# One due time and nineteen of twenty-eight lines of TensorE's written order in a window attention kernel

## The chip, the core and the metric

The kernel runs on one core of a Trainium2 chip. A core has a matrix engine (TensorE, PE in the profile, with its weight loads as PEld), a vector engine (VectorE, DVE), an engine for activation functions (ScalarE, ACT), a general engine (GpSimd, POOL) and a sequencer that here only issues transfers (SyncE, SP). They run side by side and wait for one another with semaphores. TensorE writes to PSUM, eight banks of 128 partitions by 512 words of 32 bits. The metric is the time of one execution on the device, in microseconds (us); lower is better.

## The reference

The input is an image of 224 x 224 points with 96 channels. The first 48 channels attend within horizontal strips of 8 rows, the last 48 within vertical strips of 8 columns. There are 28 strips each way, each of 1792 points.

```python
qkv = einsum('bhwc,cd->bhwd', x, wqkv)          # q, k, v of 96 channels
# first 48 channels: windows of 8 rows
ah = softmax(einsum('bqc,bkc->bqk', qh, kh) * 48 ** -0.5)
oh = einsum('bqk,bkc->bqc', ah, vh)
# last 48 channels: windows of 8 columns
av = softmax(einsum('bqc,bkc->bqk', qv, kv) * 48 ** -0.5)
ov = einsum('bqk,bkc->bqc', av, vv)
o = einsum('bhwc,cd->bhwd', concat(oh, ov), wo)
```

## The kernel before, in words

**Tiles.** The kernel takes two strips at a time: a pair `P`, 0 to 13 for rows and 14 to 27 for columns (`NPH` is 14, so pair 14 is the first column pair). In a pair the queries are cut into chunks `c` of 512, 512, 512 and 256, the keys into 14 groups of 128. A tile is 128 keys by 512 queries of both strips, 1024 columns; a pair has 14 + 14 + 14 + 7 = 49 tiles. Keys stand on the partitions, so the exponentials of a tile go into the next product as they are, and a column of ones beside the values gives the sum that softmax divides by.

**Two ways to an exponential.** 40 or 41 tiles of a pair have it taken by ScalarE (line 876, one instruction for a tile, 1126 in all). Their scores go by turns into banks 0, 1 and banks 2, 3, so TensorE can write the scores of a tile only after ScalarE has read the tile two before it. The other 8 or 9 tiles of a pair (246 in all) go through a polynomial: VectorE reads the scores (line 1003, for some tiles also 1005), GpSimd squares (lines 1016, 1019, 1020), TensorE computes the same scores a second time, and VectorE puts the result together (line 1008). These scores lie in the ring, banks 4 to 7, which also holds the sum over the values that is being added up, the projections and the output products.

**The written order.** TensorE runs its steps in the order of 28 strings, `ORDER`, one for each pair; the string of pair P is line 46 + P. A letter is a step:

- `q`: the scores of the next tile for ScalarE (line 700, 4 matmuls);
- `1`, `3`: the first scores of a polynomial tile, `2`, `4` the second (line 713). `3` and `4` take two neighbouring banks of the ring and VectorE reads both in one instruction of 1024 columns; `1` and `2` take any two banks and VectorE reads them with two instructions of 512;
- `v`: one tile of exponentials times the values (line 726), summed in one ring bank over a chunk; VectorE then copies the sum out (line 893);
- `k`: a step that prepares a pair ahead: its keys (lines 530 and 535), a small product for a bias of the queries (557 and 561), its queries (530 and 544) and its values (575 and 582); `K` is two such steps with one copy;
- `g`: an output product of the column half (lines 644 and 650); `f`: one of the last pair (611, 618 and 623).

Steps `q`, `1` to `4` and `f` are said to be of one kind here, `v`, `k` and `g` of the other, because TensorE takes longer from a step of one kind to one of the other.

**Who orders the rest.** A planner in the kernel's own program goes through the letters, keeps a time for each engine, and so decides the order of VectorE's, GpSimd's and SyncE's instructions (`dve_step`, `pool_step`, `do_s`, `do_fill`). It only sets the order. On the chip each engine runs its list in that order and each instruction waits by semaphore for what it reads and overwrites.

**The sums turned over.** Of a column pair the sums lie with channels on the partitions. After the copies of chunks 1 and 3 of a column pair, `turn_ot` (line 424) puts a transposing transfer on SyncE's queue: the first turned part has 8 groups of 128 points, the second 6. When the planner thinks that a part has landed, it gives VectorE the reciprocals of the sums of that part (`emit_rn`, line 965; 16 columns for the first part, 12 for the second), and after that GpSimd the multiplication (line 980). The second part's `turn_ot` stands in SyncE's queue behind the transfers that are queued at the start of the next pair: `rows_in` (line 444) and `plan_x` (line 465, the points of the pair after the next). The due time is this line:

```python
dq.append(dict(what="rn", ready=tm["sp"] + TURN, dur=0.16 if c == 1 else 0.135, P=P, z=c // 2))
```

`TURN` is 4.5 us; `c == 1` is the first part, `c == 3` the second.

Of the kernel before, what the change touches and what calls it, by code (L numbers as in the profile page):

```python
# [44 lines left out]
ORDER = [
    "qqkkkqkq3q1qkq1qkqkqvv3qvvq1qvqkqvvq2vq2vq3qkvqvqvvkq2qkkqvvvv1qkvqv1qkvqvkq4vqvvq4vqvkq4vqkq1vvqkqkvkqv1qvq2vqvkkv",
    "qq2vvq1qvvqvvq1vqvvvq1qvvqvvvqvq2vqkvvqkq2vq4qvvkq1vqvqvkvvq1qkvqvv2qvvq4vqvkq4qvvkq3qkvvq1qvkvqvqv2qvvqvkvq3qvkvvq1qkvvv",
    "q2vq2qvq1vqvvqvvvq1vq1qvvqvvvq4qvkqv4qvkqv4qvkqv3qkvqvvvqkvq1q4vqkvvq3qkvq2qkvq2qvkqv1qvvqvvqv4qvvkq1qvvvqkvq4vqvkvq1v",
    "q2qvvq1vqvvqvvvvq1vqv1qvqvqkq4vqkvq1vqvkvqvvq4qvvvkq2qvv1qvvq2qvvq1vkq4qvvkq3qvqkvqvvq1vvq4qvkqv3qvvvq2qkvqkkvqv2qkvqv2",
    "qvvq1vqvvqvvq2vvqv2qvvq1vqvq4vkqvq1vqkvqvvqkq1vkqvvqvvq2vqkvvqkq3vvqkq2vqkq2vq3qkvq1qvvqvvq1qvv3qkqvv2qvvqkvqvkvq2vq",  # L50
    "v1qvqvvvq2vqq1vvqvv1qvvqvqv2qq4vqvkq1vqvvvqvq1vqkvkqkvvq2kqv3qkvqv4qvvqkq1vqvvvqkqvv4qvqkv2qvvq2vqv1qvq4vqvvqkvkvq1qkvvq2v",
    "vq1qvvqvvq1vvqvq1vqvvqvv3qvvqvvqvkq2qv1qvqkv2qkvqvq2vvq1qkvvvq2kqq4vqvkq1vvqkqvvq4qkvqv1qvq4vkqvq3vkqvvq3qkvqvvqvvkvq",
    "2qvv1qvvq2vq3qvvqvvqvvq1vqvvvqkqvkvq1qvvkqv2qkvqv2qkvvq1vqv4qvkqvvq2vq4qvvkq1qvkvqvvqv2qvvq2qvv3qvkqv1qvvqkvq4vqvkvq4qvvvkq1",
    "qvvqvvq2vvqvvq1vq2qvvvq1qvvqvq1vkqvvqvkqvkqv2qkvqv2qkq1vqvvq2vqv2qvkvqkq1vqv1qvqvvvqv1qkqvvvq1qkvq2qvkqv2qvvvq1kqvvqk",
    "vqvvq2vvq4qvvvvq1vqvq4vqvkq1qvvqvvvq2vqv1qvvqvkqvkqvvvq2q1qvvq1vvqkvq2vkqv3qkvqvvqvqkq4vqkq3vqvvq4vqkvqk2qvvq1vqvvkq2qkv",
    "vq1vqvvvqq2vqvvq1vvqvvqkkq4qvkqv3qvkvqvqvvkq4vqkq1vqvkqvvq3qkvqv1qvqkvkq2qvvq2vvq2qvvq1vqvvvqv1qvvq2qvvq4vqkvq4vqvkvq1v",
    "vq1qvvvqvvqv1qvq2vvq3qvvqvvqkq1vqvvvqv2qkqvv2qkqkvvq2vkqv3qvvqv3qvkqvq2vvq2qvkqkvq1qvkqvvvqvvq3vqkvq4vqkvq2qvv2qvvq3vqvkv",
    "q1vqvqvvqvkvq2vqv1qvvq1qvkqvvvq2qvvq1vqkqvvvq2qvq3kqvq1vkqvkq2qvkqvkq2vqv4qvkqv1qvvqvvvq4qvvvqk3qkqvv4qkvqv2qvq1vkqv1",
    "qvvqvvq1qvv1qvqvvvq4qvvvqv4qvqkv2qvq1vqvvqvkqkvq3vqkvq1kvq2qvvvq4qkvvqv1qkvqvqvvq2vvq1qvkqv2qkvqvvvq3vqvkqkq2vvq1qkvvqvv",
    "qv2qvvq1vvq3qvvvqv2qvq2qvvkq2vqvv1qkvqvqv3qvvvvq4qkvvvqkvq2kqvv3qvkqvqvkqv3qvvkq4qvvvkq2qvvvq1vqvkqv1qkvvqvvq1qvvvq2qkvvvq4qvvvvq",  # L60
    "1qvvvvggqqkvvkq4vqkvq1vkqvkq4qvvvq4qvgqv3qvkqvvq2kqvgvqv1qvq2vqv3qkvqvvvqvgq1qv1qvvgqgq2qkvvq2qvgvqvkq1vqvgqvvqv2qvkqvvvq2vqk",
    "vvq1vqgvq1qvv2q2qvqvv1qvvqvgqkqvkvq4qkvqvvgq1vkqvvqk3qvgq3qvvvqvkqvq2vvq2qvvvq2qvv3qvqk4qvvqkqkvq2qvkgqvkq3qvgvqv1qkvqv",
    "vq2qvvqggqvvvq1gqvvvq3qvvkq2q4qvvvkvq1qvvvvqvq1vvq1qvkgqvkqv2qkvqggqvkq2vvq1qvvvqvkvq4qvkqv4qvvvq3qkvvvq4qkvvvqkq1vvq4qvvkvq3q",
    "vvvqvvgqvq1vvq1qvv2qvqgvgqkq2vvqkkqv2qvkqvgq1vvqvvqv3qvvqk4qvvqkvq4vqvgvq4qvvkq1qvvqvvq1vqvvvq1vvq2qvgvqkq2vqkkqkvvqkvgq1qvvvqvvqv",
    "1qvvq2vqvvgq3vqkvq4qkvvq3qkvvqvvqvkvq4vqvkq1qkvvq4qvvvqkq4vqvgvq4vqgvq3vqvkq1vqvvqgvqkqvvq4kvqvq1vqgkvqv2qkvqv2qvvgqv1qvvqv",
    "2qgvqv1qgvqvvvq1qvvvq1vqkvq2vqkqkgvqv2qvkqgvq3vkqvqvvvq4qkvvq3qvkqv4qvkqv1qkvqvgq2vqv4qvkqvvq1vqvgqvqvv3qgvqv2qvvq2qvkqkv",
    "vq3vqvvq1vqvqvv1qvvqkkqkq2qgvvq4qgvvq4vqvgq3vqvqk2vqq1vqvvqvkvq3qgvvq1vvq1qvvvqvkvqv2qkqvv2qvqkkqvq21qkqvvqkvq2vvq3qkv",
    "vqg2qvvvq1qvvvqvvqv1qvvq2vqvvq2vkqvkqv2qkqkvvvq1kqvgq2qkvqvv3qgqvvqvvvq3qgvvq4qgvvq3qkvqvvqkvq4qvvgq3qvvgq4qkvqkkqvvq1vvq1qkv",
    "vqvvq2vqvvq3vqvgvq2qvvq1vqv2qvvq3vqvvqvkvqv2qvvq2qvv1qvvq3vqvgvqvkqKqvgq1vqvvqvv2qkqv2qkvvqgkqv1qkqvvvq2kqvvq2qvvkq2qvvkkq",
    "vq1gvqvvq2vq3qvvqvvvqvvq3qgvq3vqvkq2vqvgvq4vqkqvv3qvgqvvqvkqvgq2vvqkvqgvq1vqkvgq2vqv1qkvqv2qvvq1vqvvqkqvvkq3qvvvkq2qvvkqkqkvv",  # L70
    "gq2qvv2qvvq2vqv3qvvqv1qvvqvvqv1qkvvqkqv3qvgqv4qvkqv2qkvvqv3qvkqvvqgvqv3qvkvqv4qkqvv4qkqvvkq4qkvvvq3qgvvvq1qkvvqvvqkvvq3qgvq",
    "2vqv2qvq4vgqvqvvq3vvgqvq1vvqqvvvq4qvvkqgq1vqv4qvkqv2qgvqv3qkvvq4qvvvq3qvvkqvvvqgq1vkqkq2vvq4qkvvq3vqkqvvqvvq1vvq2qvkqkvkqvkgvq2",
    "qvvvq1vqvggqvvq1qvvvqvq1vvqv2qvvq1vqv2qvvq4vqvgvq1qvvvqgvvqq2vfqvvvfq3qvvqgv4qvvfqv2qvfqgvqgvvq3vqvfqvvqvvqfv2qvvq2vfqvvfqvgqvgqfffqvvvvvvvfgff",
]
# [1411 lines left out]
```

## Time and profile before

| | |
|---|---|
| median of 3 executions | 1055.9 us (1054.55 to 1061.33) |
| the execution that was profiled | 1056.15 us |
| its span, first to last instruction | 1054.3 us |
| outside the span (1056.15 - 1054.3) | 1.85 us |
| ScalarE busy | 1042.2 us, 99% |
| TensorE busy | 1026.2 us, 97% |
| VectorE busy | 1014.9 us, 96% |
| GpSimd busy | 975.7 us, 93% |
| ScalarE's exponentials | 1126, busy 1037.1 us, idle before them 3.4 us |

Busy is the time with at least one instruction running on that engine. Matmuls overlap and their ends are modelled, so the 97% of TensorE do not mean that it had no room. A view of instructions in order of time gives for each row the start, the time it covers and, in brackets, how long the engine had been idle and whose result ended that; consecutive instructions without a gap are merged into one row with their count.

### The profile page before, as it was taken

How to read it: one execution, taken by the hardware profiler on the slowest of the kernel's cores; microseconds unless marked ns; L12 is line 12 of the kernel's file. 1: busy time of each engine (PE TensorE's matmuls, PEld its weight loads, DVE VectorE, ACT ScalarE, POOL GpSimd, SP SyncE). 2: the span in 40 equal slices, each digit the busy share in tenths (PEclk: the TensorE clock that was granted, in tenths of full speed). 3: DMA queues.
4: the chain of work that ended last, by engine and by line, in shares of the span. 5: the costliest groups of instructions: out<-in, count | busy, mean ns of one | idle time of the engine just before them, and what ended most of it. 6: DMA issues, size and time to landing. Idle time of an engine off the chain costs nothing.

```text
span 1054.3 us, 32697 instructions
## 1 busy us (share of the span) xinstructions
PE 1026.2 (97%) x13436; PEld 385.8 (37%) x13436; DVE 1014.9 (96%) x1738; ACT 1042.2 (99%) x1137; POOL 975.7 (93%) x644
## 2 busy tenths in 40 slices
...
GB/s 197 167 132 140 92 71 136 125 81 87 145 102 52 139 117 43 55 59 58 28 77 107 75 64 107 75 81 101 103 52 95 88 92 53 106 106 44 78 71 73
DMA packets 413750, 96.84 MB, mean 92 GB/s; under 512 B 404416, under 2 KB 410784, under 8 KB 413600
## 3 DMA queue, kind: packets, MB, share of 16 engines
...
q10 hardware_dynamic: 544, 0.44, 0.1%
...
q0 software_dynamic: 256, 0.39, 0.1%
...
## 4 chain that ended last, share of the span: by engine, by line
PE 54%; ACT 29%; DVE 9%; issue 6%; POOL 1%; DMA 1%; ACTq 0%; DVEq 0%
ACT PT L876 29%; PE ps L700 20%; PE ps L726 20%; PE ps L713 7%; PE ps L530 3%; DVE qb L1003 3%; DVE PT L1008 3%; PE ps L575 2%; DVE PT L1005 1%; PE ps L644 1%; DVE KT_sb L535 1%; DMA OT_tr<-OT_sb 1%; DVE OT_sb L893 1%; DVE og L650 1%; DVE QT_sb L544 0%
## 5 line engine op out<-in xcount | busy, mean ns | idle before, releaser
L876 ACT ACTIVATE PT<-ps 128x1024 bf16<-128x1024 f32 x1126 | 1037.1, 1086 | 3.4 <-PE ps L700 2.1
L1016 POOL TENSOR_TENSOR PT<-PT 128x1024 f16<-128x1024 f16 x246 | 461.8, 1894 | 20.3 <-DVE PT L1005 12.2
L700 PE MATMUL ps<-QT_sb,KT_sb 49*64 49x512 bf16 (+1 forms) x5312 | 460.5, 362 | 16.6 <-ACT PT L876 9.3
L726 PE MATMUL ps<-PT,V_sb 128*49 128x512 bf16 (+1 forms) x3136 | 461.3, 361 | 0.3 <-DVE OT_sb L893 0.2
L1008 DVE SCALAR_TENSOR_TENSOR PT<-ps,PT 128x512 uint16<-128x512 f32 (+1 forms) x407 | 312.3, 796 | 13.5 <-PE ps L713 8.4
L1003 DVE TENSOR_SCALAR qb<-ps 128x512 f16<-128x512 int16 (+1 forms) x413 | 312.9, 787 | 12.1 <-PE ps L713 7.7
L1019 POOL TENSOR_TENSOR PT<-qb 128x1024 f16<-128x1024 f16 x148 | 279.3, 1894 | 32.5 <-DVE qb L1003 23.7
L700 PEld LDWEIGHTS ps<-QT_sb,KT_sb 49*64 49x64 bf16 x5312 | 135.6, 103 | 306.9 <-ACT PT L876 284.9
L726 PEld LDWEIGHTS ps<-PT,V_sb 128*49 128x49 bf16 x3136 | 134.8, 103 | 204.4 <-issue 168.8
L713 PE MATMUL ps<-QT_sb,KT_sb 53*64 53x512 bf16 (+1 forms) x1968 | 196.9, 390 | 4.3 <-DVE PT L1008 0.7
L1020 POOL TENSOR_SCALAR PT<-PT 128x1024 f16<-128x1024 f16 x148 | 154.7, 1046 | 12.5
L1005 DVE SCALAR_TENSOR_TENSOR PT<-ps,qb 128x512 f16<-128x512 int16 (+1 forms) x172 | 125.5, 755 | 0.2
L713 PEld LDWEIGHTS ps<-QT_sb,KT_sb 53*64 53x64 bf16 (+1 forms) x1968 | 55.8, 103 | 75.6 <-DVE PT L1008 22.9
L893 DVE CAST OT_sb<-ps 113x512 bf16<-113x512 f32 x111 | 68.5, 617 | 0.6 <-PE ps L726 0.4
L544 DVE CAST QT_sb<-ps 128x512 bf16<-128x512 f32 (+1 forms) x111 | 66.9, 611 | 0.6 <-PE ps L530 0.3
L535 DVE TENSOR_SCALAR_CACHE_REDUCE KT_sb<-ps 128x512 bf16<-128x512 f32 x106 | 64.1, 616 | 0.9 <-PE ps L530 0.8
L582 DVE CAST V_sb<-ps 128x480 bf16<-128x480 f32 (+1 forms) x84 | 51.6, 618 | 0.8 <-PE ps L575 0.4
L650 DVE CAST og<-ps 128x480 bf16<-128x480 f32 x83 | 50.7, 616 | 1.2 <-PE ps L644 0.6
L530 PE MATMUL ps<-xT_sb,wq_sb 97*64 97x512 bf16 x224 | 40.7, 366 | 0.2
L530 PE MATMUL ps<-xT_sb,w_sb 97*64 97x512 bf16 x224 | 40.4, 366 | 0.1
L575 PEld LDWEIGHTS ps<-w_sb,xT_sb 96*64 96x64 bf16 x1568 | 33.5, 112 | 18.9 <-issue 5.9
L575 PE MATMUL ps<-w_sb,xT_sb 96*64 96x48 bf16 x1568 | 39.3, 190 | 0.9 <-DVE QT_sb L544 0.9
...
## 6 DMA issues: line engine op xcount, KB each, us to landing
...
out_dram<-og SPq DMA_DIRECT2D x186, 48.0 KB, 2.0
...
```

What stands on the lines that cost most here:

```text
L530: ins = e.matmul(bk[64 * w:64 * w + 64, 0:qs], lhsT=lw, rhs=xT_sb[b][0:C + 1, w, q0:q0 + qs], start=True, stop=True)
L575: ins = e.matmul(bk[64 * h:64 * h + 64, j * C2:(j + 1) * C2], lhsT=xT_sb[b][0:C, w, t0:t0 + 64], rhs=w_sb[0:C, wblk(P, "v"), 0:C2], start= ...
L700: ins = e.matmul(bank(SETS[s] + w)[64 * kh:64 * kh + 64, i * t["qs"]:(i + 1) * t["qs"]], lhsT=KT_sb[b][64 * w:64 * w + CA, kt * 128 + 64 * ...
L713: ins = e.matmul(bank(bp[w])[64 * kh:64 * kh + 64, 0:512], lhsT=KT_sb[b][64 * w:64 * w + nr, kt * 128 + 64 * kh:kt * 128 + 64 * kh + 64], ...
L726: ins = e.matmul(bank(pb)[64 * w:64 * w + CA, 0:t["qs"]], lhsT=V_sb[b][:, w, kt, :], rhs=PT[slot][:, ca:ca + t["qs"]], start=st and i == 0 ...
L876: S.commit("act", 0.0, D_ACT, None, lambda e, s=s, slot=slot: e.activation(PT[slot][:], ps[:, 512 * SETS[s]:512 * SETS[s] + 1024], ACTF.Ex ...
L1003: fn, reads, writes = lambda e: e.tensor_scalar(q, l, m, a, ALU.mult, ALU.add), bk, qk
L1005: fn, reads, writes = lambda e: e.scalar_tensor_tensor(y.bitcast(FP16), l, -RA * 2.0 ** 16, q, ALU.add, ALU.mult), bk + qk, ptk
L1008: fn, reads, writes = lambda e: e.scalar_tensor_tensor(y.bitcast(U16), f, 128.0, y.bitcast(FP16), ALU.mult, ALU.add), bk + ptk, ptk
L1016: square = ("pool", D_SQ, lambda e: e.tensor_tensor(y, y, y, ALU.mult), yk + ["pser"], yk)
L1019: return [("pool", D_SQ, lambda e: e.tensor_tensor(y, q, q, ALU.mult), qk, yk), ("pool", D_AF, lambda e: e.tensor_scalar(y, y, -(QS * (RB ...
L1020: ("pool", D_AF, lambda e: e.tensor_scalar(y, y, -(QS * (RB + RA) / 2) ** 2, 1.0, ALU.add, ALU.mult), yk + ["pser"], yk),
```

## The change

A constant is added and used in one place, and 19 of the 28 strings are replaced; pairs 2, 9, 11, 12, 17, 19, 22, 23 and 25 keep theirs. With `XTURN` the planner holds the reciprocals of the first turned part of pair 14 for 2.2 us more before it gives them to VectorE. Lines behind the constant move down by one. Shown are the strings of pairs 0, 14, 15, 20 and 27.

```diff
+XTURN = 2.2
...
 ORDER = [
-    "qqkkkqkq3q1qkq1qkqkqvv3qvvq1qvqkqvvq2vq2vq3qkvqvqvvkq2qkkqvvvv1qkvqv1qkvqvkq4vqvvq4vqvkq4vqkq1vvqkqkvkqv1qvq2vqvkkv",
+    "qqkkkqkq3q1qkq1qkqkqvv3qvvq1qvqvqkvq2vq2qv3qvkqvqvkvq2qkkqvqvkq1vq1qkvvqvvkvq2qvkvvq2qv1qvq2vqkkqvqkvkvq1qvvvkvq2vk",
...
-    "qv2qvvq1vvq3qvvvqv2qvq2qvvkq2vqvv1qkvqvqv3qvvvvq4qkvvvqkvq2kqvv3qvkqvqvkqv3qvvkq4qvvvkq2qvvvq1vqvkqv1qkvvqvvq1qvvvq2qkvvvq4qvvvvq",
-    "1qvvvvggqqkvvkq4vqkvq1vkqvkq4qvvvq4qvgqv3qvkqvvq2kqvgvqv1qvq2vqv3qkvqvvvqvgq1qv1qvvgqgq2qkvvq2qvgvqvkq1vqvgqvvqv2qvkqvvvq2vqk",
+    "3qvvq2qvq1vvqvq2vvvq2qvvvkq2qvvqkkqv1qkvvqvvkqv1qvvq2vqvvvqkq2kqvvvq1qvkvqvqkvvq1vqv2qvvq4vqvvq1vvq1qkvvqvvv2qqvvvv3qkqvv3qvvqvkvq",
+    "4qvvgvq4qvvkqq1vvqvvqv4qvgqvkq2vqgvqkgvq2vkqv3qvvqvkq1vqv4qkqvvgq3qkvqvvkqvkqv1qvvqg2qvqv4qvvgq3qgvvq1vqvqvvq2vvqkkvqvqgv2q",
...
-    "2qgvqv1qgvqvvvq1qvvvq1vqkvq2vqkqkgvqv2qvkqgvq3vkqvqvvvq4qkvvq3qvkqv4qvkqv1qkvqvgq2vqv4qvkqvvq1vqvgqvqvv3qgvqv2qvvq2qvkqkv",
+    "4qvgqv3qgvqvvvqvvq3vqkvq3qvkvq4vqvkqkvq2gvqvq3kqvvqkqv3qvvvqvgq4vqkvq4qvgvq4qvvkq1qv4qvkqv3qvvqvvvqvgq1qvv2qkqvvkqkgqv2q",
...
-    "qvvvq1vqvggqvvq1qvvvqvq1vvqv2qvvq1vqv2qvvq4vqvgvq1qvvvqgvvqq2vfqvvvfq3qvvqgv4qvvfqv2qvfqgvqgvvq3vqvfqvvqvvqfv2qvvq2vfqvvfqvgqvgqfffqvvvvvvvfgff",
+    "qvvgvqv1qvvq1vqvvqgvqvvq1vvq2qvvvq1vqgvq2vqv4qvvqgv1qvvqvvq1qvvvqgfqvv4qvvfqvvq4qfvvq4vqvgqv1qvfqvvvqvvfqvfqv4qvgqv4qvvfqvvfqgvqvffqvvgvvffvgff",
 ]
...
-                    dq.append(dict(what="rn", ready=tm["sp"] + TURN, dur=0.16 if c == 1 else 0.135, P=P, z=c // 2))
+                    dq.append(dict(what="rn", ready=tm["sp"] + TURN + (XTURN if (P, c) == (NPH, 1) else 0.0), dur=0.16 if c == 1 else 0.135, P=P, z=c // 2))
```

The work stays the same: 1126 tiles for ScalarE, 246 polynomial tiles, the same matmuls for scores and values. In all strings together there are 3 letters fewer of `1` and 3 more of `3`, 5 fewer of `2` and 5 more of `4`, and one more `K` in place of two `k`. In the instruction lists that follow from it, three stretches of SyncE's queue have another order (around pair 5 the transfers that keep a row pair's results go behind the loads of the next points; as pair 16 begins, the first transposing transfer of pair 15's joined channels, `turn_cat`, goes ahead of `rows_in` and `plan_x`; near the end two stores go ahead of such a transfer), GpSimd's multiplications move by an instruction or two at a few places, and at the end ScalarE takes over one output copy of 480 columns from VectorE.

More of the change, by code (lines that the diff above doesn't have):

```diff
@@ L52 @@
[L52 to L54 removed]
+    "q2qvvq1vqvvqvvvq1vqv1qvvqvqkq4vqkvq1vqvkvqvvq4qvvvkq2qvv1qvvq2vqvq1vkq4qvvkq3qvqvkqvvq1vvq4qvkqv3qvvvq2qkvqkkvqv2qkvqv2",
@@ new lines @@
+    "qvvq1vqvvqvvq2vvqv2qvvq1vqvq4vkqvq1vqkvqvvqkq1vkqvvqvvq2vqkvvqkq3vvqkq2vqkq2vq3qkvq1qvvqvvq1qvv3qvkqv2qvvqkvqvkvq2vq",
+    "1qvvqvvvq2vqv1qvvq1vqvqvvq2vqv2qvqKkqvvq1qvvvqvvq2vkqvq1vkqvkq3vqkvvq4qkvvq1qvvvqvvq4vqkvq2qvkqvkq2vqvvq4vqkvvq1vqv2qvvq1",
+    "vvq1qvvvqvq3vqvvq1vqvvvqv1qvvqvvqv4qvkq2qkqvv2qvvq3vqkvq3qvvqk2qvv2qkvq1qkvqvvvqkvq4qkqv4qkvqv3qvkqvv1qvvq3qvvkqvvqkvq2v",
+    "qv2qvvq1vvqvq1vqvvvqvq3vqvvqvkqvvkq2vqv4qvkqv1qkqv2qkvq3vvqkq4vqkvq4vqvkqkq1vqvvqvv2qkqvvq2vvq1qvvvqkvq2vqv1qvvvq4qvvvkq1",
@@ L55 @@
+    "vqvqvvq2vqvvvq1vqv2qvvq1qvvqvq1vkqvvqvkqvkqv2qkvqv2qkq1vqvvq2vqv2qvkvqkq1vqv1qvqvvvqv1qkqvvvq1qkvq2qvkqv2qvvvq1kqvvqk",
     "vqvvq2vvq4qvvvvq1vqvq4vqvkq1qvvqvvvq2vqv1qvvqvkqvkqvvvq2q1qvvq1vvqkvq2vkqv3qkvqvvqvqkq4vqkq3vqvvq4vqkvqk2qvvq1vqvvkq2qkv",
-    "vq1vqvvvqq2vqvvq1vvqvvqkkq4qvkqv3qvkvqvqvvkq4vqkq1vqvkqvvq3qkvqv1qvqkvkq2qvvq2vvq2qvvq1vqvvvqv1qvvq2qvvq4vqkvq4vqvkvq1v",
+    "vq1vqvvvqq2vqvvq1vvqvvqkkq4qvkqv3qvkvqvqvvkq4vqkq1vqvkqvvq3qkvqv1qvqkvkq2qvvq2vvq2qvvq1vqvvvqv1qvvqv2qvq4vqkvq4vqvkvq1v",
@@ L63 @@
+    "4qvvgvq4qkvvqkq1vvqvvqv4qvgqvkq2vqgvqkgvq2vkqv3qvvqvkq1vqv4qkqvvgq3qkvqvvqkvqkv1qvvqg2qvqv4qvvgq3qgvvq1vqvqvvq2vvqkkvqvqgv2q",
+    "vgqv1qvvq1vqv2q2qvqvv1qvvqvgqkqvkvq4qkvqvvgq1vkqvvqk3qvgq3qvvvqvkqvq2vvq2qvvvq2qvv3qvqk4qvvqkqkvq2qvkgqvkq3qvgvqv1qkvqv",
     "vq2qvvqggqvvvq1gqvvvq3qvvkq2q4qvvvkvq1qvvvvqvq1vvq1qvkgqvkqv2qkvqggqvkq2vvq1qvvvqvkvq4qvkqv4qvvvq3qkvvvq4qkvvvqkq1vvq4qvvkvq3q",
-    "vvvqvvgqvq1vvq1qvv2qvqgvgqkq2vvqkkqv2qvkqvgq1vvqvvqv3qvvqk4qvvqkvq4vqvgvq4qvvkq1qvvqvvq1vqvvvq1vvq2qvgvqkq2vqkkqkvvqkvgq1qvvvqvvqv",
+    "vvvqvvgqvq1vvq1qvv2qvqgvgqkq2vvqkkqv2qvkqvgq1vvqvvqv3qvvqk4qvvqkvq4vqvgvq4qvvkq1qvvqvvq1vvqvvq1vvq2qvgvqkq2vqkkqkvvqkvgq1qvvvqvvqv",
```

14 lines of the change are left out of this document (5 added, 9 removed).

## The prediction

> **What bounds the kernel.** I began with the page's first and fifth parts (busy times, costliest groups) and then went through ScalarE alone in order of time.
>
> ```profile
> span 1054.3 us, 32697 instructions
> PE 1026.2 (97%) x13436; PEld 385.8 (37%) x13436; DVE 1014.9 (96%) x1738; ACT 1042.2 (99%) x1137; POOL 975.7 (93%) x644
> L876 ACT ACTIVATE PT<-ps 128x1024 bf16<-128x1024 f32 x1126 | 1037.1, 1086 | 3.4 <-PE ps L700 2.1
> L700 PEld LDWEIGHTS ps<-QT_sb,KT_sb 49*64 49x64 bf16 x5312 | 135.6, 103 | 306.9 <-ACT PT L876 284.9
> ```
>
> Four engines look full, so busy shares decide nothing. The last two rows do: ScalarE's exponentials had 3.4 us of idle time ahead of them in the whole run, while TensorE's weight loads for their scores waited 284.9 us for ScalarE. ScalarE sets the pace and TensorE has room. In order of time, ScalarE's exponentials are a few unbroken runs:
>
> ```profile
> 8.42 22.32 ACT L876 ACTIVATE PT<-ps 128x1024 bf16<-128x1024 f32 x24
> 31.33 532.99 ACT L876 ACTIVATE PT<-ps 128x1024 bf16<-128x1024 f32 x579 [0.59 <-PE ps L700]
> 564.68 12.97 ACT L876 ACTIVATE PT<-ps 128x1024 bf16<-128x1024 f32 x14 [0.36 <-PE ps L700]
> 578.28 1.02 ACT L876 ACTIVATE PT<-ps 128x1024 bf16<-128x1024 f32 x1 [0.64 <-PE ps L700]
> 579.60 69.10 ACT L876 ACTIVATE PT<-ps 128x1024 bf16<-128x1024 f32 x75 [0.29 <-PE ps L700]
> 648.97 19.68 ACT L876 ACTIVATE PT<-ps 128x1024 bf16<-128x1024 f32 x21 [0.27 <-POOL PT L1020]
> 668.83 379.97 ACT L876 ACTIVATE PT<-ps 128x1024 bf16<-128x1024 f32 x412 [0.18 <-PE ps L700]
> 1049.30 0.38 ACT L1327 ACTIVATE OT_sb<-ps 113x256 bf16<-113x256 f32 x1 [0.50 <-PE ps L726]
> ```
>
> The same view of pair 2 alone gives the pace when nothing is late:
>
> ```profile
> 84.00 36.78 ACT L876 ACTIVATE PT<-ps 128x1024 bf16<-128x1024 f32 x40
> ```
>
> One exponential by itself takes 1.02 us (the row at 578.28), so 39 more take 36.78 - 1.02 = 35.76 us, 0.917 us each. 1126 at that pace need 1125 x 0.917 + 1.02 = 1032.6 us. They ran from 8.42 to 668.83 + 379.97 = 1048.80, 1040.4 us, which is 7.8 us more. Of these, 2.3 are the bracketed gaps (0.59 + 0.36 + 0.64 + 0.29 + 0.27 + 0.18); the other 5.5 are delays too short for a bracket, inside the runs. Ahead lie 8.4 us of start, behind 1054.3 - 1048.8 = 5.5 us of end. **So the order of steps can give back 7.8 us at most, 0.7%,** plus what it changes at the two ends.
>
> The Trainium skill, "ScalarE: Activation LUTs", section "What ACT_TABLE_LOAD costs", gives an ACTIVATE with immediates 186 ns + 0.833 ns an element and lets neighbours overlap by about 93 ns, which would be 946 ns for 1024 elements and, as an estimate from it, 1065 us for 1126. The trace disagrees (0.917 us each, and a span below that), so the room of 7.8 us stands.
>
> **The change part by part.**
>
> *The due time.* The rows of the two turned parts of pair 14, from SyncE's transfers (two windows of the view of that tile, and SyncE in order of time), VectorE and GpSimd:
>
> ```profile
> 552.52 1.27 SPq L418 DMA_TRANSPOSE OT_tr<-OT_sb  x1
> DMA to landing us min/median/max: 3.0/3.0/3.0
> 559.32 0.24 DVE L965 RECIPROCAL rn<-OT_tr 128x16 f32<-128x16 bf16 x1
> 574.83 1.48 POOL L980 TENSOR_TENSOR stg<-OT_tr,rn 128x768 bf16<-128x768 bf16 x1
> ...
> 565.98 0.59 SPq L291 DMA_DIRECT2D stg<-oh_all  x1
> 566.61 2.99 SPq L291 DMA_DIRECT2D xT_sb<-xt_dram  x2
> 569.70 1.24 SPq L418 DMA_TRANSPOSE OT_tr<-OT_sb  x1
> DMA to landing us min/median/max: 6.8/6.8/6.8
> 576.57 0.23 DVE L965 RECIPROCAL rn<-OT_tr 128x12 f32<-128x12 bf16 x1 [1.07 <-DMA OT_tr<-OT_sb]
> ```
>
> The first part (16 columns) landed at 552.52 + 3.0 = 555.5; its reciprocal ran at 559.3, 3.8 us later, without a wait, and GpSimd used the result 15 us after that. Holding it for 2.2 us more takes nothing away and delays nobody: 0 us. Its cover is GpSimd's 15 us; without it the price would be 2.2 us of GpSimd, not of ScalarE. **The reciprocal that VectorE did wait for is that of the second part** (12 columns, 1.07 us), and its due time is not touched. Its transfer stands on SyncE behind `rows_in` and `plan_x`, and landed 6.8 us after its issue, not 3.0.
>
> *What that wait cost, and costs now.* Behind it came a copy of queries, behind that TensorE's values step for its bank, behind that a `q`:
>
> ```profile
> 576.71 0.63 DVE L544 CAST QT_sb<-ps 128x512 bf16<-128x512 f32 x1
> ...
> 574.05 0.40 PE L700 MATMUL ps<-QT_sb,KT_sb 49*64 49x512 bf16 x4
> 574.95 0.41 PE L700 MATMUL ps<-QT_sb,KT_sb 49*64 49x512 bf16 x4
> 577.39 0.50 PE L575 MATMUL ps<-w_sb,xT_sb 96*64 96x48 bf16 x20 [0.90 <-DVE QT_sb L544]
> 577.82 0.41 PE L700 MATMUL ps<-QT_sb,KT_sb 49*64 49x512 bf16 x4
> ```
>
> That `q` at 577.82 is the exponential at 578.28 (0.46 later): ScalarE lost 0.64 + 0.29 = 0.93 us. In the new lists VectorE has, at this place, the first half of a `2`, the same reciprocal, the small reduction for the bias, the second half of that `2`, the copy of a sum. TensorE's order is `2 v k q v 3 q`. In both strings the sums of pair 14 end at the same `q` (the 603rd), so I keep the times of before: the `2` falls between the `q` at 574.05 and that at 574.95, its first half is read by about 575.4, and the reciprocal then waits for 576.54 (569.70 + 6.84, quoted as 6.8) again. The `3` needs two neighbouring banks of a ring whose four are held by the sum, the two halves and the reduction. It starts after the reduction (about 576.9) or after the second half (one more 0.61, 577.5); its `q` is 0.24 later, at 577.1 to 577.7, where 577.0 would have been in time (577.0 + 0.46 is the next start at the undisturbed pace, 577.5). That is 0.1 to 0.7 us lost, against 0.93. I take 0.5: **gain 0.4**, ends 0.8 gained and, if the transfer lands later, a loss (the first rival).
>
> *The bunches of steps.* Between two `q` TensorE can hold about 1.83 - 0.46 = 1.37 us of work (two paces, less the way from `q` to exponential). The strings of before have, the end of the last aside, three gaps longer than that by a count of letters, at 0.23 us a step (the four `v` from 562.77 to 563.70 below) and some 0.1 more for a change of kind: `vvvv1` after the 24th `q`, `vvvvgg` after the 603rd and `vvvkv` after the 693rd. In the trace:
>
> ```profile
> 29.52 1.05 PE L726 MATMUL ps<-PT,V_sb 128*49 128x512 bf16 x8
> 30.65 0.41 PE L713 MATMUL ps<-QT_sb,KT_sb 50*64 50x512 bf16 x4
> 30.89 0.39 PE L700 MATMUL ps<-QT_sb,KT_sb 49*64 49x512 bf16 x4
> ...
> 562.77 1.09 PE L726 MATMUL ps<-PT,V_sb 128*49 128x256 bf16 x16
> 563.70 0.59 PE L644 MATMUL ps<-wo,oc_all 96*64 96x96 bf16 x20
> 564.22 0.63 PE L700 MATMUL ps<-QT_sb,KT_sb 49*64 49x512 bf16 x8
> ```
>
> Each is one of ScalarE's gaps: 0.59 ahead of 31.33, 0.36 ahead of 564.68, and 0.27 ahead of 648.97. The new strings lose the first two (0.95 us) and keep the third (pair 17 is unchanged). They have two new ones of that length, `vvvkv` after the 40th `q` and `vvvv3` after the 597th. The nearest rows price them at 0.27 (the same letters) to 0.59; I take 0.3 each. **Gain 0.95 - 0.6 = 0.35**, ends 0.4 gained and 0.25 lost.
>
> *The other strings.* They move delays inside the 5.5 us that have no bracket; two thirds of the pairs (19 of 28) are changed, so 3.7 us stand to be won, and as much to be lost if the new orders hold twice as many. No row prices one against the other, and unchanged and changed pairs look alike; I take 0.
>
> *Edits with the answer 0.* Eight more polynomial reads of 1024 columns (3 more `3`, 5 more `4`) save 0.07 us each (1.22 against 1.29 below), VectorE's and not ScalarE's. TensorE changes kind 1924 times, not 1910, 1.5 us in all beside the 284.9 us that its loads wait. SyncE's three swaps concern transfers used a pair later; if that cover went, 1 to 3 us would show at one place. At the end ScalarE's new copy of 480 columns fits beside TensorE's last sum, in the 0.50 us ahead of 1049.30, or delays it by 0.1.
>
> ```profile
> 580.27 1.29 DVE L1003 TENSOR_SCALAR qb<-ps 128x512 f16<-128x512 int16 x2
> 582.82 1.22 DVE L1003 TENSOR_SCALAR qb<-ps 128x1024 f16<-128x1024 int16 x1
> ```
>
> **Sum.** 0.4 + 0.35 + 0 = 0.75 us less: the profiled execution's 1056.15 becomes 1055.4. The median of the runs shown is 1055.9, 0.25 below that execution, so I say 1055.1.
>
> **The rivals.**
>
> *The second part comes later and `3` pays: slower.* The transfer hangs on a chain that begins with the reciprocals and multiplications of pair 13:
>
> ```profile
> 548.69 0.32 DVE L965 RECIPROCAL rn<-OT_tr 128x28 f32<-128x28 bf16 x1
> 550.74 1.31 POOL L980 TENSOR_TENSOR ohn<-OT_tr,rn 128x672 bf16<-128x672 bf16 x1
> 552.14 1.04 POOL L1020 TENSOR_SCALAR PT<-PT 128x1024 f16<-128x1024 f16 x1
> 553.26 1.31 POOL L980 TENSOR_TENSOR ohn<-OT_tr,rn 128x672 bf16<-128x672 bf16 x1
> ```
>
> From the end of the second (554.57) it is 15.1 us to the issue at 569.70, all transfers one behind the other. In the new order that reciprocal comes behind one more copy of values and one more polynomial half (some 0.6 us each, like the copy at 576.71), up to 1.2 us later; the second multiplication has one GpSimd instruction fewer ahead of it (1.04), so the chain may shift by -1 to +1.2. With +1.2 the `3` costs 0.7 + 1.2 = 1.9 instead of 0.93, and if the two new bunches cost 0.59 each, another 0.25 is lost: +1.2 us, 1057.1; with a doubled wait at one more such place, 1059. It decides from a landing after about 577. The Trainium skill, "DMA: Bandwidth & Descriptors", section "Queues, rings and completion order", says that each DMA engine consumes descriptors in ring order for what one sequencer issues; by that rule the transfer stays behind `plan_x`'s loads whatever VectorE's due time is, and the trace agrees (6.8 against 3.0 us). Against this rival: the shift may as well be negative.
>
> *It does nothing.* The held reciprocal was not late, the wait stays at 0.93, and the new bunches cost what the old did: 1055.9, within 0.3.
>
> *The search wins inside the runs.* Half of the 3.7 us, the wait and the bunches: 1055.9 - 1.85 - 0.93 - 0.35 = 1052.8. For it: 5.5 us of short delays lie open to another order. Against it: nothing in the rows says that the planner sees them.
>
> **How the numbers follow.** Forecast 0.45 (own range 1053.9 to 1056.0), slower 0.27 (1056.2 to 1060, likeliest 1057.1), nothing 0.18, the larger gain 0.10 (down to 1051.5). The range 1052.5 to 1059.5 leaves out less than 2 in 10. About 1% (10.6 us) is what a measurement of this kernel can tell from no change; 10.6 us faster is more than the 7.8 there are (0.01), 10.6 slower needs a chain of waits that no row shows (0.04).
>
> **What would show it.** Right: no gap of ScalarE after the 24th exponential or near 564; VectorE's reciprocal of 12 columns near 576 still with a bracket naming the transfer, that of 16 without one; a `3` behind it; ScalarE's runs ending 0.5 to 1 us earlier. Wrong: that bracket gone, new ScalarE gaps at the 41st and 598th exponential above 0.6, or a bracket naming a transfer elsewhere.

## The result, and the profile after

| | before | after |
|---|---|---|
| median | 1055.82 us (22 executions, 1054.53 to 1061.33) | 1053.86 us (22 executions, 1053.38 to 1054.58) |
| profiled execution, span | 1056.15, 1054.3 us | 1053.98, 1052.2 us |
| ratio of the times, after to before | | 0.998, 95% interval 0.9974 to 0.9987 |

The change takes 1.96 us off, 0.2%: very little, but with an interval that leaves 1 out. A gain of 0.75 us was forecast, from 1055.9 to 1055.1 us.

The page of after, its first part and the first row of its costliest groups:

```profile
span 1052.2 us, 32693 instructions
PE 1026.2 (98%) x13436; PEld 386.5 (37%) x13436; DVE 1013.7 (96%) x1728; ACT 1042.1 (99%) x1138; POOL 974.1 (93%) x642
L877 ACT ACTIVATE PT<-ps 128x1024 bf16<-128x1024 f32 x1126 | 1036.6, 1087 | 2.1 <-PE ps L701 0.8
```

No engine is less busy in a way that matters. ScalarE's idle time ahead of its exponentials fell from 3.4 to 2.1 us. ScalarE of after in order of time (start, time covered, in brackets the gap ahead and whose result ended it):

```profile
8.51 21.33 ACT L877 ACTIVATE PT<-ps 128x1024 bf16<-128x1024 f32 x23 [0.16 <-PE ps L701]
30.18 526.21 ACT L877 ACTIVATE PT<-ps 128x1024 bf16<-128x1024 f32 x572 [0.34 <-PE ps L701]
556.54 90.49 ACT L877 ACTIVATE PT<-ps 128x1024 bf16<-128x1024 f32 x98 [0.15 <-PE ps L701]
647.30 360.92 ACT L877 ACTIVATE PT<-ps 128x1024 bf16<-128x1024 f32 x391 [0.27 <-DVE PT L1009]
1008.38 38.63 ACT L877 ACTIVATE PT<-ps 128x1024 bf16<-128x1024 f32 x42 [0.16 <-PE ps L701]
1047.68 0.38 ACT L1328 ACTIVATE OT_sb<-ps 113x256 bf16<-113x256 f32 x1 [0.20 <-PE ps L727]
```

From 563 to 592 there is now no gap at all, where before stood 0.36, 0.64 and 0.29. VectorE and SyncE's queue at that place, in order of time:

```profile
574.34 0.69 DVE L1009 SCALAR_TENSOR_TENSOR PT<-ps,PT 128x512 uint16<-128x512 f32 x1
574.95 0.22 DVE L966 RECIPROCAL rn<-OT_tr 128x12 f32<-128x12 bf16 x1
...
569.37 1.24 SPq L419 DMA_TRANSPOSE OT_tr<-OT_sb  x1
```

and, from the view of the tile `OT_tr` there, the time from that issue to its landing:

```profile
DMA to landing us min/median/max: 5.5/5.5/5.5
```

**The wait of 1.07 us is gone, although the reciprocal now stands earlier (574.95, not 576.57).** The transfer was issued 0.33 us earlier than before (569.37 against 569.70) and landed 1.66 earlier (574.88 against 576.54): 5.5 us after its issue, not 6.8.

Where did the rest come from? I take for each exponential the time from the end of the one ahead to its own end, less the undisturbed pace (0.9167 us, quoted as 0.917), and add this excess up by pairs. Before it is 8.07 us in all, after 6.20. The pairs that moved most:

| pair | 0 | 1 | 5 | 15 | 18 | 20 | 25 | others together |
|---|---|---|---|---|---|---|---|---|
| before | 1.01 | 0.33 | 0.33 | 1.72 | 0.45 | 0.39 | 0.19 | 3.65 |
| after | 1.17 | 0.43 | 0.02 | 0.33 | 0.67 | 0.04 | 0.30 | 3.24 |

Pairs 5, 15 and 20 carry it in these two profiles. Their rows (40 exponentials and the one ahead; undisturbed 41 take 40 x 0.917 + 1.02 = 37.70), before first, then after:

```profile
193.43 38.02 ACT L876 ACTIVATE PT<-ps 128x1024 bf16<-128x1024 f32 x41
749.92 38.18 ACT L876 ACTIVATE PT<-ps 128x1024 bf16<-128x1024 f32 x41
```

```profile
193.58 37.82 ACT L877 ACTIVATE PT<-ps 128x1024 bf16<-128x1024 f32 x41
562.14 38.02 ACT L877 ACTIVATE PT<-ps 128x1024 bf16<-128x1024 f32 x41
748.47 37.77 ACT L877 ACTIVATE PT<-ps 128x1024 bf16<-128x1024 f32 x41
```

Pair 15 took 39.41 us before (562.38 to 601.79), 1.39 more than now. Of its excess before, 0.74 + 0.40 lay directly behind the reciprocal and 0.47 behind `vvvvgg`; that last place has 0.16 now. The ends of the two spans (behind the last exponential) are 5.48 and 5.18 us, the starts 8.42 and 8.51.

**Why the transfer landed earlier.** It comes in 16 shares. In before, 15 landed from 574.88 to 575.15, and one at 576.54. In after all 16 landed from 574.56 to 574.88. The view of the transfer queues, taken in slices of 0.02 us, shows what ran beside. The first fence is before, its two rows from the slices at 574.44 and at 575.56; the second is after, from the slice at 574.08. A row gives packets, MB, and their share of 16 engines' time in the slice, counting the whole length of packets that start in it:

```profile
q8 instruction: 1, 0.02, 351.6%
...
q1 hardware_dynamic: 2, 0.00, 8.1%
```

```profile
q8 instruction: 1, 0.02, 333.8%
q1 hardware_dynamic: 23, 0.00, 112.5%
```

The packet of q8 carries 16 KB of program and takes 351.6% x 16 x 0.02 = 1.125 us on its DMA engine: from 574.44 to 575.57. The page of the profile counts 105 of them in a run. TensorE's 13436 + 13436 instructions make 256 for each of them (26872 / 105 = 255.9), so I take them for TensorE's program; no view names the engine. In before the last two packets of the transfer start at 575.564 and 575.571, as that block ends. In after the block (574.09 to 575.16) comes at the same moment of the transfer, but all packets of the transfer had started by 574.13, and from 574.95 to 576.5 none starts. So the same two transfers meet in both kernels; in one a share stands behind the block, in the other none does.

### The profile page after: what moved, and what is told of

It is laid out like the page before. It is cut to its first block, busy times and chain, and to the rows that moved or that the text cites. A ratio compares the mean times of both kernels' runs of the same rounds, so it can differ in the third digit from the quotient of the medians.

```text
span 1052.2 us, 32693 instructions
## 1 busy us (share of the span) xinstructions
PE 1026.2 (98%) x13436; PEld 386.5 (37%) x13436; DVE 1013.7 (96%) x1728; ACT 1042.1 (99%) x1138; POOL 974.1 (93%) x642
## 3 DMA queue, kind: packets, MB, share of 16 engines
q8 instruction: 105, 1.72, 0.7%
## 4 chain that ended last, share of the span: by engine, by line
PE 52%; ACT 27%; DVE 10%; issue 7%; POOL 3%; ACTq 0%; DVEq 0%; POOLq 0%
ACT PT L877 27%; PE ps L727 19%; PE ps L701 19%; PE ps L714 7%; DVE qb L1004 3%; PE ps L531 3%; DVE PT L1009 3%; PE ps L576 1%; POOL PT L1020 1%; POOL PT L1017 1%; PE ps L645 1%; DVE PT L1006 1%; DVE QT_sb L545 1%; DVE OT_sb L894 1%; DVE KT_sb L536 0%
```

## The experiments

Theory A: the gain is mostly the wait behind that late share, and any small shift of the two transfers against each other decides it. Theory B: the gain sits where the strings were changed. Each expectation says in its own words what its theories mean there. Comparisons are with runs of the kernel before on the same chip (medians 1055.85, 1055.89 and 1055.83 us).

### The due time alone, and the strings alone

```diff
+XTURN = 2.2
-                    dq.append(dict(what="rn", ready=tm["sp"] + TURN, ...
+                    dq.append(dict(what="rn", ready=tm["sp"] + TURN + (XTURN if (P, c) == (NPH, 1) else 0.0), ...
```

> The strings of before with the new constant: one VectorE instruction, the reciprocal of the first part's 16 columns in pair 14, runs four instructions later, and nothing else moves. Theory 'due time' (the gain comes from the constant): about 1 us faster. Theory 'order' and theory 'block' (the wait for the second part, 12 columns, came from one of the 16 shares of its transfer, which had to wait for a block of TensorE's own instructions being loaded): within 0.3 us of before, the 12 columns' wait of 1 us still there if the block falls at the same moment.

Measured: 1055.55 us, ratio 0.9995 (0.9986 to 1.0004), as the theories 'order' and 'block' said. VectorE's row still has the wait:

```profile
576.47 0.23 DVE L966 RECIPROCAL rn<-OT_tr 128x12 f32<-128x12 bf16 x1 [0.83 <-DMA OT_tr<-OT_sb]
```

The other half, all 19 strings of after without the constant:

> The strings of after without the new constant: the reciprocal of the 16 columns runs one instruction earlier than in after. Theory 'due time': 1 us slower than after, about 1054.9. Theories 'order' and 'block': as after, 1053.9 plus or minus 0.3.

Measured: 1054.04 us, ratio 0.9981 (0.9972 to 0.999), no wait. The constant does nothing that can be measured; the strings make the difference.

### The strings of pairs 14 and 15, and all others

> The strings of before but for those of pairs 14 and 15, which are after's; without the constant. From the delays of ScalarE counted pair by pair in the two traces (pairs 14 and 15: 2.29 us in before, 0.93 in after): 1.4 us faster than before, 1054.4. Theory 'search everywhere': at most 0.5 us faster, since 17 of the 19 strings are missing.

> The strings of after but for those of pairs 14 and 15, which are before's; without the constant. From the delays pair by pair (the other pairs 0.5 us less in after) and the end (0.3 us shorter): 0.7 us faster than before, 1055.1. Theory 'search everywhere': 1.5 us or more. If theory 'block' holds, the 12 columns' wait can come or go here, as TensorE's instructions ahead of it are the same in number but 0.6 us earlier: with the wait 1055.1, without it 1054.2.

Measured: pairs 14 and 15 alone 1054.59 us, ratio 0.9989 (0.998 to 0.9998), 1.26 less; all others without these two 1053.80 us, 0.9982 (0.9974 to 0.9991), 2.05 less. The first is near what its own pairs promised (1.4), the second 0.4 more than was expected of it without the wait (1054.2), and as much as 'search everywhere' asked. **Each half gives most of the whole,** and together they would be 3.3, not 1.96. What both have in common is that the late share is gone, in the second even with the old strings of pairs 14 and 15. In that kernel the reciprocal stands at 574.75 without a bracket, and the 16 shares landed from 573.62 to 573.94.

### The wait taken out of the kernel before by itself

First by SyncE's queue: the loads of pair 17's points go behind the second turned part of pair 14.

```diff
-            elif P >= NPH - 1 and P + 1 < NP:
+            elif P >= NPH - 1 and P + 1 < NP and P != NPH + 2:
                 plan_x(P + 1)
...
                     turn_ot(P, c // 2)
+                    if (P, c) == (NPH, 3):
+                        plan_x(NPH + 3)
```

> The kernel before, with one change on SyncE's queue: the second turned part of pair 14 goes ahead of the two loads of pair 17's points instead of behind them. Theory A (the wait for that part costs what it costs because one of the transfer's 16 shares is held up by a block of TensorE's program): the transfer lands near 572, before the block of 574.4 begins, VectorE's reciprocal of 12 columns has no wait, and ScalarE's 0.64 + 0.29 behind it go: 0.9 to 1.1 us less than before, about 1054.8. Theory B (the gain of the change lies in the order of TensorE's steps, the wait is hidden by something else): no wait either, but the time stays at 1055.8 within 0.3. Whether it is the block or the place in the queue that makes the transfer late, this run does not tell.

Then by the due time of the reciprocal that waits:

```diff
-... ready=tm["sp"] + TURN, dur=0.16 ...
+... ready=tm["sp"] + TURN + (2.2 if (P, c) == (NPH, 3) else 0.0), dur=0.16 ...
```

> The kernel before, with VectorE's reciprocal of the second turned part (12 columns, the one that waits) held by 2.2 us in the planner, as the change does for the first part (16 columns): on VectorE it moves behind a copy of queries, a copy of sums and a few more. The transfer and the blocks stay as they were and the last share still lands near 576.5. Theory A and its price (a wait of 1.07 on VectorE, 0.93 lost by ScalarE): the reciprocal comes after the landing, has no wait, and the time is 0.8 to 1.0 us less, about 1054.9. Theory B (the wait costs nothing of the end): 1055.8 within 0.3.

Measured: 1055.36 us, ratio 0.9997 (0.9988 to 1.0005), and 1055.32 us, 0.9995 (0.9986 to 1.0003): 0.53 and 0.57 less, half to two thirds of what was expected. The steps came out as said. In the first the transfer landed by 573.12, and the reciprocal at 576.36 has no wait; in the second the last share is late again (576.83), and the reciprocal comes behind it. VectorE and ScalarE of the second:

```profile
577.75 0.22 DVE L965 RECIPROCAL rn<-OT_tr 128x12 f32<-128x12 bf16 x1
...
565.27 35.85 ACT L876 ACTIVATE PT<-ps 128x1024 bf16<-128x1024 f32 x39 [0.44 <-PE ps L700]
```

No gap is left behind the reciprocal, and the excess of pair 15 fell from 1.72 to 0.65 and 0.54. But both profiles have 0.46 to 0.48 more excess in pair 0, whose instructions are the same. That place varies by itself: the profile of before, with 1.01, is the lowest of eight with this string. But one profile each can't say why the medians of 11 executions gained no more, and the lowest of these executions (1055.19 and 1054.94) are slower than the quick ones of the kernel before (1054.72 and 1054.89 among the 35 on this chip). So these two runs leave open whether the wait is worth 0.55 us of the time or 1.1.

### The blocks of program moved

TensorE writes the scores of six tiles twice (24 matmuls and 24 weight loads more, the same values): ahead of the place, so that the blocks come earlier, and behind it as the control, which has 768, 790, 812, 835, 846 and 858 in `AGAIN`.

```diff
-NTW0, NTWICE = 1, 6
+NTW0, NTWICE = 1, 6; AGAIN = (416, 434, 445, 463, 476, 488)
...
-... qk_fn(tl, s, 2 if NTW0 <= ia[0] <= NTWICE else 1) ...
+... qk_fn(tl, s, 2 if NTW0 <= ia[0] <= NTWICE or ia[0] in AGAIN else 1) ...
```

> The kernel before, where TensorE writes the scores of six tiles of pairs 10 and 11 twice (24 matmuls more, the same values), so that from there on the blocks of its program are fetched about 48 instructions earlier, which is some 1.9 us. No list of VectorE, GpSimd, ScalarE or SyncE changes, and the transfer keeps its place behind the loads. Theory A (a block holds up one share): the block starts near 572.5 instead of 574.4, all 16 shares land by about 575.2, VectorE's reciprocal of 12 columns loses its wait of 1.07 and ScalarE the 0.93 behind it: 0.8 to 1.1 us less, about 1054.9, if the repeats themselves cost nothing (TensorE waits for ScalarE at those places). Rival (the transfer lands at 6.8 us because it stands behind the loads): the wait stays, 1055.8 or up to 0.5 more for the repeats.

> The control for the run with earlier blocks: the same six repeats of scores in the kernel before, but at six tiles of pairs 18 to 21, behind the place of the wait. The blocks up to 574 stay where they were. Both theories: the wait of about 1 us on the reciprocal of 12 columns remains in most executions, 1055.8 within 0.3, up to 0.5 more if repeats cost something. If this run is about 1 us faster too, the repeats and not the blocks make the gain, and theory A falls.

Measured, earlier blocks: 1056.61 us (1055.62 to 1070.53), ratio 1.0034 (1.0011 to 1.0057). That is the rival's time (the wait stays, up to 0.5 more for the repeats), not what theory A said: the seven executions with a mean clock of 0.999 or 1.000 took 1055.62 to 1056.66 us. The other five, with a mean clock from 0.984 to 0.994, took 1061.80 to 1070.53; none of those was profiled. In the profile the block fell at 570.73, among the loads ahead of the transfer, and took 2.02 us instead of 1.1. No share was late by itself, but all 16 landed from 576.09 to 576.33, and the wait stayed, at 0.81:

```profile
576.36 0.23 DVE L965 RECIPROCAL rn<-OT_tr 128x12 f32<-128x12 bf16 x1 [0.81 <-DMA OT_tr<-OT_sb]
```

So the experiment didn't free the transfer of the block, it let the block meet the loads instead, and theory A's cause is not tested by it. The control: 1055.81 us (1054.50 to 1056.10), 0.9998 (0.9989 to 1.0006), as expected. Its profiled execution was its quickest, 1054.50, and has no late share (all between 574.24 and 574.51) and no wait, with the order ahead of 600 us unchanged. Against the profile of before it is 1.65 us shorter: 1.0 of this is pair 15, 0.47 the start and 0.33 the end, while other places lost 0.15. The kernel before itself has two groups of times: 9 of 125 executions beside these experiments lie between 1054.37 and 1054.89, the others at 1055.28 and above. That the first group is the one without the late share fits this profile, but only one such execution was profiled.

### The early strings and the late strings

> The kernel before with the new strings of pairs 0 to 13 alone. ScalarE's own loss there can be read from the changed kernel: 0.3 us less in pair 5, pair 0 unsettled (+0.2 to -0.3). Theory A (the transfer's last share is late by accident, and any shift of the place where a block of TensorE's program is fetched against the transfer decides it): VectorE's wait on the reciprocal of 12 columns may go, although pairs 14 and 15 are untouched; then the time is near 1054.5 (0.3 + about 1.1 less), with the wait it is near 1055.5. Rival (the gain sits where the strings are changed): 1055.5, with the wait of about 1 us still there.

> The kernel before with the new strings of pairs 16 to 27 alone. Nothing ahead of 600 us is touched, so under each theory the wait on the reciprocal of 12 columns stays as in the kernel before. What the later strings give is then seen alone: from the changed kernel's rows 0.35 in pair 20, 0.1 elsewhere and 0.3 at the end, so 1055.1 (0.5 to 0.9 less than before). If it is 1.5 or more less, the wait is not where the gain comes from; if 0.2 or less, it is the wait and pair 5 alone.

Measured: pairs 0 to 13 alone 1055.21 us, 0.62 less, ratio 0.9998 (0.9988 to 1.0007), with one execution at 1060.18 and a mean clock of 0.995, and four of the 12 at 1053.78 to 1054.87; pairs 16 to 27 alone 1054.68 us, 1.15 less, 0.999 (0.9981 to 0.9998), although no order ahead of 600 us is touched in it. In both, pairs 14 and 15 run the same instructions in the same order. ScalarE and VectorE with the early strings:

```profile
561.07 2.96 ACT L876 ACTIVATE PT<-ps 128x1024 bf16<-128x1024 f32 x3
564.47 12.94 ACT L876 ACTIVATE PT<-ps 128x1024 bf16<-128x1024 f32 x14 [0.44 <-PE ps L700]
578.02 1.02 ACT L876 ACTIVATE PT<-ps 128x1024 bf16<-128x1024 f32 x1 [0.62 <-PE ps L700]
579.49 22.11 ACT L876 ACTIVATE PT<-ps 128x1024 bf16<-128x1024 f32 x24 [0.44 <-PE ps L700]
...
576.30 0.23 DVE L965 RECIPROCAL rn<-OT_tr 128x12 f32<-128x12 bf16 x1 [1.07 <-DMA OT_tr<-OT_sb]
```

and with the late strings:

```profile
561.51 2.96 ACT L876 ACTIVATE PT<-ps 128x1024 bf16<-128x1024 f32 x3
564.88 36.99 ACT L876 ACTIVATE PT<-ps 128x1024 bf16<-128x1024 f32 x40 [0.41 <-DVE OT_sb L893]
...
575.67 0.22 DVE L965 RECIPROCAL rn<-OT_tr 128x12 f32<-128x12 bf16 x1
```

The expectation for the late strings, that the wait stays, did not hold in this profile. This is the cleanest pair: the same list at this place, with and without the late share (last landings 576.28 and 574.81). Pair 15's excess is 1.81 and 0.73, so **by this pair of profiles the wait costs ScalarE 1.08 us at this place**. The same comparison can be made of all 14 profiles of this study, since a pair's string is the old one in some and the new one in others. Mean excess of a pair (lowest to highest), in us:

| pair | old string | new string | difference |
|---|---|---|---|
| 15, with the wait on VectorE | 1.65 (1.49 to 1.81), 4 profiles | | |
| 15, without it | 0.67 (0.54 to 0.73), 5 profiles | 0.25 (0.20 to 0.33), 4 profiles | -0.42 |
| 5 | 0.31 (0.24 to 0.40), 8 profiles | 0.05 (0.00 to 0.11), 6 profiles | -0.26 |
| 20 | 0.19 (0.01 to 0.41), 8 profiles | 0.03 (0.00 to 0.04), 6 profiles | -0.16 |
| 0 | 1.31 (1.01 to 1.49), 8 profiles | 1.16 (0.98 to 1.37), 5 profiles | -0.15 |
| 3 | 0.35 (0.31 to 0.42), 8 profiles | 0.24 (0.19 to 0.30), 6 profiles | -0.11 |
| 18 | 0.43 (0.19 to 0.57), 8 profiles | 0.54 (0.31 to 0.68), 5 profiles | +0.11 |

So the wait is worth 1.65 - 0.67 = 0.98 us of pair 15, and of the 0.35 that pair 20 showed above half was luck in the two profiles. The 0.3 at the end isn't the change either: it took 5.47 us with the new last strings here, and 5.15 in the control with the old ones.

### A longer wait put into the kernel after

```diff
-... (XTURN if (P, c) == (NPH, 1) else 0.0) ...
+... (XTURN if (P, c) == (NPH, 1) else -1.4 if (P, c) == (NPH, 3) else 0.0) ...
```

> The changed kernel, where VectorE gets the reciprocal of the second turned part (12 columns) two instructions earlier, ahead of a copy of keys and a combination for a polynomial tile; the transfer, the blocks and TensorE's order are as they were. VectorE then stands from about 573.4 to 574.9, a wait of 1.4 us that the changed kernel doesn't have. Theory A with its price (0.93 of ScalarE for 1.07 of VectorE, as in the kernel before): 1.2 us more than the changed kernel, 1055.1. Theory B (such a wait on VectorE is hidden, the gain came from elsewhere): 1053.9 within 0.3. Half the price (0.6 more, 1054.5) would fit the two runs that took the wait out of the kernel before and gained 0.55.

Measured: 1064.86 us (1055.40 to 1069.67), ratio 1.0069 (1.004 to 1.0097). Far more than any theory said, and not by the wait itself. VectorE and TensorE in order of time:

```profile
576.02 0.23 DVE L966 RECIPROCAL rn<-OT_tr 128x12 f32<-128x12 bf16 x1 [2.14 <-DMA OT_tr<-OT_sb]
...
576.60 0.41 PE L714 MATMUL ps<-QT_sb,KT_sb 53*64 53x512 bf16 x4 [2.09 <-DVE KT_sb L536]
```

The view by stretches (from and to, length; busy time and count of PE, PEld, DVE, ACT and POOL; granted clock of TensorE; DMA share and GB/s):

```profile
574.00:576.00 2.00, 0.50 (x6) 0.11 (x4) 0.00 (x0) 1.67 (x2) 2.00 (x2) 1.00 0.55 93
576.00:577.00 1.00, 0.41 (x6) 0.18 (x6) 0.98 (x4) 0.00 (x0) 1.00 (x1) 0.98 0.00 0
577.00:578.00 1.00, 1.00 (x12) 0.50 (x10) 1.00 (x4) 0.00 (x0) 1.00 (x2) 0.50 0.00 0
578.00:590.00 12.00, 12.00 (x102) 3.48 (x100) 7.05 (x10) 7.96 (x8) 7.06 (x6) 0.50 0.42 78
590.00:592.00 2.00, 2.00 (x34) 0.94 (x34) 2.00 (x3) 1.83 (x3) 2.00 (x2) 0.85 0.00 0
```

TensorE stood still for 2.09 us behind VectorE, and from 576.97 to 590.62, 13.65 us, it had half its clock. In this time TensorE, otherwise with room, seems to set the pace: 102 matmuls and 8 instructions of ScalarE are counted from 578 to 590, where the kernel after has 182 and 15:

```profile
578.00:590.00 12.00, 11.83 (x182) 4.68 (x184) 11.75 (x18) 12.00 (x15) 11.76 (x8) 1.00 0.49 92
```

Pair 15's excess is 7.80 us in this execution (1061.99 us, mean clock 0.993), in which the last share was late as well, by 0.6 us (575.42 and 576.00). Nine of the 12 executions have a mean clock from 0.983 to 0.998; the three at 1.000 take 1055.40 to 1055.67, which is 1.5 to 1.8 more than the kernel after. None of these three was profiled. If their wait was between the planned 1.4 and the 2.14 of the profile, that is nearer to the full price than to half of it. That VectorE's wait reaches ScalarE's end is thus shown; its price without the clock is only bounded.

### Shorter runs of steps

The kernel after with seven of its remaining bunches split, here three of them:

```diff
-...vkvq2qkkqvqvkq1vq1q...       (pair 0)
+...vkvq2qkqkvqvkq1vq1q...
-...q4qvvvkvq1qvvvvqvq1...       (pair 17)
+...q4qvvkqvv1qvvvqvvq1...
-...qkvkqvkgvq2                  (pair 26)
+...qkvkqvkgqv2
```

> The changed kernel with seven of the places evened out where ScalarE still has an excess: in pair 0 the double k after the 22nd q and the long strings at the end of the pair (with the first letters of pair 1), in pair 17 the vvvkv with the vvvv behind it and a kvvv, at the start of pair 18 a vvg, in pair 26 a 3vvg and the vkgv at its end. No letter is added or lost. These places cost ScalarE 0.45, 0.55, 0.38, 0.23, 0.19, 0.20 and 0.27 us in the changed kernel's trace, 2.3 in all. Theory (a bunch of steps between two q is what costs ScalarE, and splitting it gives the loss back): half to two thirds of it, 1.1 to 1.5 us less than the changed kernel, about 1052.6. Rival (what is won at one place is lost at the next, since TensorE, VectorE and the ring's banks are as full as ScalarE): 1053.8 within 0.3.

Measured: 1055.21 us (1054.96 to 1055.56), 1.35 more than the kernel after (the two ran on different chips); ratio to before 0.9995 (0.9986 to 1.0004). The rival's direction holds, and the loss is larger than it said (1053.8). Of the pairs that were split some lost excess (pair 0 from 1.17 to 0.85, pair 26 from 0.52 to 0.29), but pair 17 went from 1.11 to 1.32, pair 1, with its first letters edited, from 0.43 to 1.30, and pair 27, which has no edit, has 0.50 where it had under 0.1. Two rows show the new gaps:

```profile
70.69 19.53 ACT L877 ACTIVATE PT<-ps 128x1024 bf16<-128x1024 f32 x21 [0.28 <-PE ps L701]
1011.32 36.84 ACT L877 ACTIVATE PT<-ps 128x1024 bf16<-128x1024 f32 x40 [0.30 <-PE ps L701]
```

The first is 24 tiles behind the edited letters: VectorE's combinations of polynomial tiles there have another order, and one waits 0.52 us for TensorE. The second is behind the `vvgv` after pair 27's first `q`, the next letters after the last edit.

## Why the prediction came out as it did

**The due time: right.** 0 us was said, 0.3 less with an interval across 0 was measured.

**The wait: wrong in its step.** "The reciprocal then waits for 576.54 again" took the 6.8 us to landing as a property of the place in SyncE's queue. The other 15 shares had landed 5.45 us after the issue (575.15 - 569.70); the rest of the 6.84 was one share of 16. The prediction's own sign of being wrong came true: the bracket on the reciprocal of 12 columns is gone. The sum put a gain of 0.4 on this term, for a `3` that waits a little less, where the wait as a whole, about 1.0 by the profiles, could go. The two loads of `plan_x` seem to delay the issue more than the way to landing: put ahead of them, the transfer still took 5.87 us (567.25 to 573.12). What was right is where the time of before was lost: VectorE's wait, then the copy of queries, then TensorE, 0.93 of ScalarE by the brackets (1.08 by the pair of profiles with the same list, 0.98 by the means). The sentence from the Trainium skill ("DMA: Bandwidth & Descriptors", "Queues, rings and completion order"), that each DMA engine consumes descriptors in ring order, held for SyncE's own transfers: in the kernel after, the two loads of points landed at 572.88 and 574.04, and the first share of the transfer at 574.56.

**The bunches: right in size for `vvvvgg` by the profiles, wrong for the others.** It was priced at 0.36 and gave 0.42. In the times this does not show: with all new strings 1054.04 us, without those of pairs 14 and 15 1053.80, on the same chip. Of the 0.59 in pair 0 only 0.15 came back: the gap went, but 0.34 stands one exponential earlier. The new `vvvkv`, priced at 0.3, shows 0.12 in the profile of after; the new `vvvv3` shows 0.07, and `vvv2`, two exponentials ahead of it, 0.26.

**The other strings: 0 was said.** Pairs 5, 20 and 3 gave 0.26, 0.16 and 0.11 in the mean, pair 18 took 0.11. The others moved by less than 0.1 each, about what the same code varies by.

**The range held, in part by luck.** The measured gain is more than twice the forecast. A larger gain was among the cases, with a chance of 0.10, and that case did count the wait as gone (0.93); but it took 1.85 of its gain from short delays in many pairs, of which pairs 5, 20 and 3 gave 0.53, and nothing in the working said why the wait should go. The first rival (a later second part) did not come. That a longer wait on VectorE reaches ScalarE is shown by the one put into the kernel after; the rival's price for it left out the clock.

The sum by the means of the profiles: 0.98 for the wait, 0.42 for `vvvvgg`, 0.53 for pairs 5, 20 and 3, 0.15 for pair 0, less 0.11 for pair 18: 1.97, against 1.96 measured. That it fits so closely is chance. The same means, added up for the other runs, give 1.40 for the strings of pairs 14 and 15 (1.26 measured), 0.52 for the early strings (0.62), 1.03 for the late ones if the wait goes (1.15), but 1.55 for all strings without 14 and 15 (2.05), and 0.98 for the two runs that took out the wait alone (0.53 and 0.57). A sum of these terms can be half a microsecond off, and with 0.55 for the wait some 0.4 of the 1.96 has no place.

**What stays open.** That the block causes the late share is argued, not shown by a run that takes the block away. For it: in the four profiles with one share a full microsecond late, the transfer's last packets start within 0.03 us of the block's end (before: 575.571 and 575.569; the due time alone: 575.333 and 575.333; the held reciprocal: 575.808 and 575.807; the early strings: 575.260 and 575.260). In a fifth, that of the longer wait, the share was late by only 0.58 us, and its last packets (575.052 and 575.058) start at the end not of the 16 KB block but of one of 8 KB on another queue, q14, which ran from 574.746 to 575.055. In all five the share is late by its block's length and 0.27 to 0.42 us more.

But a meeting is not enough. In twelve of the 14 profiles (all but those of the run with earlier blocks and of the run with the transfer ahead of the loads) the 16 KB block starts from 4.68 to 4.76 us after the transfer's issue, although this issue moved from 568.44 to 570.16, and within 0.05 us of the transfer's last packets in time. Seven of the twelve have no late share, and the spacing doesn't tell them from the others: 4.71 to 4.76 without, 4.68 to 4.75 with. So a shift of the two against each other, as theory A had it, is not what decides, as far as these traces resolve it. In all twelve they meet; what decides whether a share is caught, and why the block keeps this spacing, isn't known. Nor is it known why the late strings, which change nothing ahead of the place, seem to have the late share more rarely: nine of their 11 executions took 1054.26 to 1054.84 us, but only one was profiled.
